# Moving transpositions and loads in a fused linear-attention and SwiGLU kernel

## The chip, the cores and the metric

The kernel runs on one core of one Trainium2 chip. The core has a TensorE (matrix multiplications, which also does transpositions by multiplying with an identity matrix), a VectorE, a ScalarE and a GpSimd engine, and a SyncE that only issues transfers. Transfers run on 16 DMA engines, which serve the queues of all issuers. In the profile's rows the engines are called PE (PEld is its loading of stationary operands), DVE, ACT, POOL and SP.

The metric is device time in microseconds; smaller is better.

## The reference

Linear attention with cosine weights, followed by a gated feed-forward network. There are 8 batches of 8 heads, 576 positions and 64 columns a head, so 4608 tokens of 512 columns; the feed-forward width is 1536.

```python
def phi(x, c, s):
    r = np.maximum(x, 0.0)
    return np.concatenate([r * c, r * s], axis=-1)
q_p = phi(q, cos_w, sin_w)
k_p = phi(k, cos_w, sin_w)
kv = np.einsum('bhsf,bhsd->bhfd', k_p, v)
z = np.sum(k_p, axis=2)
num = np.einsum('bhsf,bhfd->bhsd', q_p, kv)
den = np.einsum('bhsf,bhf->bhs', q_p, z)[..., None] + 1e-06
attn = num / den                       # then x: one row of 512 a token

rms = np.sqrt(np.mean(x * x, axis=-1, keepdims=True) + 1e-06)
xn = x / rms * rms_g
g = xn @ w_gate
out = (g * (1.0 / (1.0 + np.exp(-g))) * (xn @ w_val)) @ w_out
```

## The kernel before

**Tiles and blocks.** The first 512 positions of batch b are block b, four x tiles of 128 tokens (j = 0 to 3). The last 64 positions of all eight batches are gathered two batches at a time ("tails", four "pairs") into block 8. The blocks run in the order 0 to 6, 8, 7.

**A block of the feed-forward network.** For each of 12 column groups n (steps 0 to 11), `gval_step` multiplies the transposed normed x (`xnT`, 512 tokens wide) with 128 columns of the gate weights into a bank `psG[n % 2]` and of the value weights into `psV[n % 2]`, four matmuls each. `gval_h` applies silu on ScalarE and multiplies on VectorE into `hT`. Then four output steps (12 to 15), `out_step`, multiply one token tile each with the output weights (12 matmuls), copy the result and store it over SP's queue.

**The attention of later batches** runs between these steps. The function `at(blk, n, where, f, *args)` puts a call into a slot of a block's step: "pe" is ahead of the step's matmuls, "mid" in the middle of an output step, "pre" after the matmuls, "post" at the end. Within a slot, calls run in the order in which they were entered; each engine and each queue works in program order. For a batch these calls are:

- `load_kv`, `load_q`: transfers from DRAM into one of five buffers `raw`. Batches 0 to 2 hold k and v in one layout, batches 3 to 7 (`wide`) in another, with all heads of 112 rows in one transfer and the last rows in a second.
- `k_phi`, `q_phi`: half of each on VectorE, half on ScalarE. `v_cast`: v to bfloat16.
- `q_tr_pe` with `q_tr_evac`, or `q_tr_dma`: q's features transposed into `qpT`, on TensorE with a copy out of the bank, or by a DMA transposition on SP's queue.
- `kvz_pe`, `kvz_evac`: the sums over positions.
- `nd_pe`, `nd_post`, `x_sq`, `x_norm`: one tile's numerator and denominator on TensorE, the division on VectorE, the mean square on ScalarE (and a power on GpSimd), the normed tile `xn` on VectorE.
- `x_tr_pe` with `x_tr_evac`, or `x_tr_dma`: `xn` transposed into `xnT`, four 128 x 128 transpositions on TensorE and a copy, or a DMA transposition on SP's queue.
- `load_q_tails`, `q_tails_phi`, `q_tails_tr_dma`, `nd_tails_pe`: the same for a pair's tails.

**Block 0** is special, since nothing is there to run behind. Its attention comes first; then the twelve column groups are worked on in eight `units`, as x tiles become ready: units 0 to 3 take tile 0 or 1 alone with four column groups each (128 tokens wide), units 4 to 7 take tiles 2 and 3 as a pair with two column groups each (256 wide). `unit_mm(i, w)` does a unit's 16 (or 8) matmuls for the gate or the value weights, `unit_silu` and `unit_h` the rest. Column groups 8 to 11 are then done for all four tiles in `gval_step`. `out_first` does the output of block 0: 48 matmuls, and after every sixth a slot, so that steps 12 to 15 with "pe" and "mid" hold batch 1's `nd_pe`, `x_norm` and transpositions (the table `X1`, lines 744 to 757). `filler` matmuls on a tile of zeros stand where TensorE would otherwise have nothing in the opening.

**Queues.** GpSimd's queue carries the opening loads: q0, v0, the weights, k1, q1, v1, and, from block 0's column steps, k2, v2 and q2. SP's queue carries k0, and from the end of block 0 on the output stores, the DMA transpositions and the loads of batch 3 on. A DMA transposition takes its place in SP's order behind the loads and stores ahead of it.

**Lines that the change and the prediction touch:** `load_kv` (106), the units (606 to 709), batch 1's x tiles (744 to 757), the loads of batch 2 (731 to 737), the tails (785 to 796), the loads of batches 3 to 7 (797 to 804).

Of the kernel before, what the change touches and what calls it, by code (L numbers as in the profile page):

```python
# [17 lines left out]
def kernel(  # L18
# [11 lines left out]
    nc = tc.nc  # L30
    B, H, S, D = q.shape
    DM = H * D
    DFF = moe_w_gate.shape[1]
    P = 128
    TB = 512
    HP = H // 2
# [4 lines left out]
    NDT = DM // P  # L41
# [5 lines left out]
    V, A, G = nc.vector, nc.scalar, nc.gpsimd  # L47
# [10 lines left out]
    psG = [ps.tile([P, 512], FP32, name=f"psG{i}") for i in range(2)]  # L58
    psV = [ps.tile([P, 512], FP32, name=f"psV{i}") for i in range(2)]
    psC = [ps.tile([P, 512], FP32, name=f"psC{i}") for i in range(2)]  # L60
# [8 lines left out]
    def kv_rows(src, b, hps):  # L69
        return src[b, 2 * hps[0] : 2 * hps[1], :, :].rearrange(  # L70
            "(hp hh) (s c) d -> (hh s) hp (c d)", hh=2, c=NC
        )

    def wide(b):
        return b > 2
# [4 lines left out]
    def kv_rows5(src, b, r0, r1):  # L80
        part = src[b, :, 0 : NC5 * (KP - 1), :].rearrange(
            "h (p c) d -> p h (c d)", c=NC5
        )[r0 : min(r1, KP - 1)]
        return bass.AP(part.tensor, part.offset, [[NC5 * D, r1 - r0]] + list(part.ap)[1:])
# [6 lines left out]
    def raw_tile(which, b):  # L91
        if (which, b) not in raw:
            t = ring.tile([P, H * NC5 * D], FP32, name="raw", tag="raw")
            raw[(which, b)] = t
        return raw[(which, b)]

    def raw_kv(which, b):
        t = raw_tile(which, b)
        if wide(b):
            return t[:, :].rearrange("p (h e) -> p h e", h=H)  # L100
        return t[:, 0 : HP * NC * D].rearrange("p (hp e) -> p hp e", hp=HP)
# [4 lines left out]
    def load_kv(which, b, hps=(0, HP), eng=nc.sync):  # L106
        src = k if which == "k" else v
        if not wide(b):
            return eng.dma_start(
                out=raw_kv(which, b)[:, hps[0] : hps[1], :], in_=kv_rows(src, b, hps)  # L110
            )
        last = KP if b < B - 1 else KP - 1
        for r0, r1 in ((0, KM), (KM, last)):
            eng.dma_start(out=raw_kv(which, b)[r0:r1, :, :], in_=kv_rows5(src, b, r0, r1))
        if last < KP:
            eng.dma_start(
                out=raw_kv(which, b)[last:KP, :, :].rearrange("p h (c d) -> p h c d", d=D),
                in_=src[b, :, S - 1 : S, :].rearrange("h s d -> s h d").unsqueeze(2)
                .to_broadcast([1, H, NC5, D]),
            )  # L120
# [19 lines left out]
    for c0, c1 in ((0, 4), (4, NC)):  # L140
        nc.sync.dma_start(
            out=raw_kv("k", 0)[:, :, c0 * D : c1 * D],
            in_=kv_rows(k, 0, (0, HP))[:, :, c0 * D : c1 * D],
# [24 lines left out]
    wg = one.tile([P, NDT, DFF], BF16, name="wg")  # L168
    wv = one.tile([P, NDT, DFF], BF16, name="wv")
# [42 lines left out]
    part, left = [], 1e-6  # L212
    for i in range(3):
        m, e = math.frexp(left)
        part.append(math.ldexp(round(m * 256), e - 8))
        left -= part[i]
        G.memset(eps_rows[32 * i : 32 * i + 32, :], part[i] / 32)
    load_kv("k", 1, eng=G)
    load_w(wg, moe_w_gate, 8, NNT)

    def g_spread(bank, t):
# [12 lines left out]
        out=th[:, 0:NTAB], in0=fidx[:, :], scalar1=S - 1.0, scalar2=ang,  # L234
        op0=ALU.min, op1=ALU.mult,
    )
    for c0, c1, less in ((0, 9, 576.0), (13, 14, 64.0)):
        V.tensor_scalar(
            out=th[64:128, c0:c1], in0=fidx[64:128, c0:c1], scalar1=-less, scalar2=ang,
# [3 lines left out]
        out=th[:, NTAB : 2 * NTAB], in0=th[:, 0:NTAB], scalar1=math.pi / 2.0,  # L243
# [4 lines left out]
        out=sel[:, :, :], in_=ident[0:4, 0:4].unsqueeze(2).to_broadcast([4, NDT, P])  # L248
# [17 lines left out]
    xnT = [one.tile([P, NDT, TB], BF16, name=f"xnT{i}") for i in range(2)]  # L266
# [6 lines left out]
    def copy(eng, o, i):  # L273
        if eng is A:
            A.copy(out=o, in_=i)  # L275
        else:
            eng.tensor_copy(out=o, in_=i)  # L277
# [201 lines left out]
    def nd_post(b, j):  # L479
        nd_rec(b, j)  # L480
        nd_div(b, j)
# [22 lines left out]
    def x_dst(b, j):  # L504
        if j == 4:
            t, col = xnT_tail, b // 2
        else:
            t, col = xnT_of(b), j
        return t[:, :, col * P : (col + 1) * P]
# [4 lines left out]
    def x_tr_pe(b, j, bank, ts=(0, NDT)):  # L514
        xn = xn_of[(b, j)]
        dst = bank.bitcast(BF16).rearrange("p (t s) -> p t s", s=P)
        for t in range(*ts):
            nc.tensor.transpose(dst[:, t, :], xn[:, t * P : (t + 1) * P], ident[:, :])

    def x_tr_evac(eng, b, j, bank, ts=(0, NDT)):  # L520
        dst = bank.bitcast(BF16).rearrange("p (t s) -> p t s", s=P)
        copy(eng, x_dst(b, j)[:, ts[0] : ts[1], :], dst[:, ts[0] : ts[1], :])
# [48 lines left out]
    def filler(n, bank):  # L571
        for _ in range(n):
            nc.tensor.matmul(
                bank[:, :], lhsT=warm[:, 0:P], rhs=warm[:, :], start=True, stop=True
            )
# [30 lines left out]
    units = [(j, j + 1, 4 * i, 4 * i + 4) for i in range(2) for j in range(2)]  # L606
    units += [(2, 4, n, n + 2) for n in range(0, 8, 2)]
    sg_of = {}

    def unit_mm(i, w, by_rows=False):  # L610
        j0, j1, n0, n1 = units[i]
        bank = (psG if w is wg else psV)[i % 2]
        width = (j1 - j0) * P
        todo = [(n, t) for n in range(n0, n1) for t in range(NDT)]
        if by_rows:
            todo = [(n, t) for t in range(NDT) for n in range(n0, n1)]
        for n, t in todo:
            nc.tensor.matmul(  # L618
                bank[:, (n - n0) * width : (n - n0 + 1) * width],
                lhsT=w[:, t, n * P : (n + 1) * P],  # L620
                rhs=xnT[0][:, t, j0 * P : j1 * P],
                start=(t == 0 and (n == n0 or not by_rows)),
                stop=(t == NDT - 1 and (n == n1 - 1 or not by_rows)),
                skip_group_check=by_rows,
            )

    def unit_silu(i):
        sg_of[i] = four.tile([P, TB], FP32, name="sg", tag="sg")
        A.activation(out=sg_of[i][:, :], in_=psG[i % 2][:, 0:TB], func=AF.Silu)

    def unit_h(i):
        j0, j1, n0, n1 = units[i]
        V.tensor_tensor(
            out=hT[:, n0:n1, j0 * P : j1 * P],
            in0=psV[i % 2][:, 0:TB].rearrange("p (n s) -> p n s", n=n1 - n0),
            in1=sg_of[i][:, :].rearrange("p (n s) -> p n s", n=n1 - n0), op=ALU.mult,
        )
# [22 lines left out]
    x_sq(0, 1)  # L660
    load_q(1, eng=G)
    load_kv("v", 1, eng=G)
    x_norm(0, 0, (0, HALF))
    x_norm(0, 0, (HALF, DM))
# [5 lines left out]
    q_tr_evac(A, 0, 3, qbank[3])  # L670
    x_norm(0, 1)
    nd_post(0, 2)
    filler(2, psG[1])
    unit_mm(0, wg, by_rows=True)
    x_tr_pe(0, 1, psC[0])
    x_tr_evac(V, 0, 1, psC[0])
    unit_mm(0, wv)
    x_sq(0, 2)
    load_wo(0, 4)
# [13 lines left out]
    x_tr_evac(V, 0, 2, psC[1])  # L693
    unit_silu(2)
    unit_h(0)
    unit_mm(3, wg)
    x_tr_pe(0, 3, psC[0])
    x_tr_evac(V, 0, 3, psC[0])
    unit_silu(3)
    unit_h(1)  # L700
    unit_mm(4, wg)
    for i in range(2, 4):
        unit_mm(i, wv)
        unit_h(i)
    unit_silu(4)
    unit_mm(5, wg)
    unit_mm(4, wv)
    unit_silu(5)
# [4 lines left out]
    def at(blk, n, where, f, *args):  # L713
        slots.setdefault((blk, n), {}).setdefault(where, []).append((f, args))
# [19 lines left out]
    at(0, 10, "post", load_kv, "v", 2, (0, HP), G)  # L734
    at(0, 12, "pe", kvz_pe, 1)
    at(0, 12, "pe", kvz_evac, A, 1)
    at(0, 11, "post", load_q, 2, (0, 4), G)

    def x_tr(b, j, bank):
        x_tr_pe(b, j, bank)  # L740
# [3 lines left out]
    X1 = (  # L744
        ((12, "mid"), (13, "pe"), (14, "pe")),
        ((13, "pe"), (13, "mid"), (14, "mid")),
        ((13, "mid"), (14, "pe"), (15, "pe")),
        ((14, "pe"), (14, "mid"), (15, "mid")),
    )
# [3 lines left out]
        if j:  # L753
            at(0, *X1[j - 1][1], x_norm, 1, j - 1)
    at(0, *X1[3][1], x_norm, 1, 3)
    for j in range(4):
        at(0, *X1[j][2], x_tr, 1, j, psV[j % 2])
    for nb in range(2, B):
        b = nb - 1
        first = nb == 2  # L760
# [16 lines left out]
        for j in range(4):  # L777
            n = ((6, 8, 10, 12) if first else (4, 6, 8, 10))[j]
# [5 lines left out]

    for pair in range(4):
        b = 2 * pair or 3
        if pair == 0:
            at(1, 15, "post", load_q_tails, 0)
        at(b, 3, "post", q_tails_phi, V, pair, 0)
        at(b, 3, "post", q_tails_phi, A, pair, 1)  # L790
        at(b, 3, "post", q_tails_tr_dma, pair)
        at(b, 12, "pe", nd_tails_pe, pair)
        at(b, 12, "pre", nd_post, 2 * pair + 1, 4)
        at(b, 12, "post", x_sq, 2 * pair + 1, 4)
        at(b, 13, "post", x_norm, 2 * pair + 1, 4)
        at(b, 13, "post", x_tr_dma, 2 * pair + 1, 4)
    for nb in range(3, B):
        b = nb - 2
        late = b == 1
        at(b, 0, "post", load_kv, "k", nb)  # L800
        at(b, 5 if late else 3, "post", load_kv, "v", nb)
        at(b, 8 if late else 6, "post", load_q, nb)
        if nb % 2 == 1:
            at(b, 9, "post", load_q_tails, nb // 2)

    def gval_step(blk, n):
        run(blk, n, "pe")
# [86 lines left out]
```

## Time and profile before

| | |
|---|---|
| median of 3 runs | 324.93 us (324.65 to 325.04) |
| profiled execution | 324.66 us |
| its span, first to last instruction | 322.9 us |
| granted clock of TensorE | 0.999 |
| transfers | 53.37 MB, mean 165 GB/s |
| out stage of block 0, first matmul | 42.87 us |
| block 1, first matmul | 55.80 us |
| block 2, first matmul | 89.22 us |

The page of a profile gives busy times by engine, the chain of work that ended last, groups of like instructions and the transfers. A timeline row has a start, a duration, the engine, the line, the operation, the tile written and those read, the shape and a count; in brackets stands how long the engine was idle before it, and what ended that. A row of stretches has the stretch, its length, the busy time and count of each engine (PE, PEld, DVE, ACT, POOL), TensorE's granted clock, the mean busy share of the DMA engines, and GB/s. A row of waits has who waited for whom, the total in microseconds, how many times, and the longest. In all of them the times are microseconds from the span's start.

Some sizes of transfers, issue to landing, by the page: loads of k, v and q on SP's queue 8.4, 8.5 and 8.9 us (1120, 1120 and 1024 KB); on GpSimd's queue 19.4, 16.1 and 16.1 us; x transpositions on SP's queue 7.8 us; output stores 2.4 us.

### The profile page before, as it was taken

What the parts mean: (1) busy time and instruction counts of PE and PEld (TensorE: products, weight loads), DVE (VectorE), ACT (ScalarE), POOL (GpSimd) and SP (SyncE); (2) the same over time, 40 slices, a digit from 0 to 9 for tenths busy, and PEclk for the clock granted to TensorE, in tenths of its full rate; (3) what the DMA queues carried; (4) which work ended last, traced back from release to release, by engine and by line L of the source; (5) the groups of instructions that cost most, each with busy time, mean ns of one, the idle gap of its engine ahead of it and who ended that gap; (6) DMA issues with size and microseconds to landing.
All of it is one profiled execution on the core that took longest, in us unless ns stands there. A gap on an engine that the chain in (4) does not pass through costs nothing.

```text
span 322.9 us, 6078 instructions
## 1 busy us (share of the span) xinstructions
PE 315.6 (98%) x2312; PEld 163.5 (51%) x2348; DVE 185.5 (57%) x380; ACT 164.9 (51%) x319; POOL 40.6 (13%) x78
## 2 busy tenths in 40 slices
PE   8999999999999999999999999999999999999996
PEld 3688565544454445444544445444544444444444
DVE  8875958767636773676457745781577034204410
ACT  5664766744665457445754575446644333223321
POOL 9771302001001100011001000110011000000000
PEclk9999999999999999999999999999999999999999
DMA  7999996999789966998699959994822300041002
GB/s 229 233 266 272 283 327 240 230 200 240 149 156 232 234 190 161 195 233 202 175 198 214 210 148 207 202 217 141 119 49 48 117 32 0 2 98 31 3 32 97
DMA packets 77627, 53.37 MB, mean 165 GB/s; under 512 B 50410, under 2 KB 71326, under 8 KB 77598
## 3 DMA queue, kind: packets, MB, share of 16 engines
q1 hardware_dynamic: 70374, 39.81, 58.2%
q0 software_dynamic: 7216, 13.17, 16.5%
q8 instruction: 18, 0.29, 0.4%
q14 instruction: 11, 0.09, 0.1%
q10 hardware_dynamic: 8, 0.00, 0.0%
HBM read 37.83 MB, written 9.44 MB: 146 GB/s over the span
## 4 chain that ended last, share of the span: by engine, by line
PE 93%; DMA 2%; DVE 2%; issue 1%; POOL 0%; ACT 0%; ACTq 0%; POOLq 0%
PE psV L528 27%; PE psC L551 27%; PE psG L528 26%; PE psA L421 2%; DMA raw<-in_q_dram 2%; PE psG L551 2%; PE psV L618 2%; PE psA L359 2%; PE psG L618 1%; PE psA L366 1%; DVE xn L499 1%; PE psV L335 0%; PE psA L446 0%; DVE xt L471 0%; PE psG L402 0%
## 5 line engine op out<-in xcount | busy, mean ns | idle before, releaser
L548 DVE TENSOR_TENSOR hT<-psV,sg 128x512 bf16<-128x512 f32 x100 | 68.9, 689 | 102.1 <-PE psV L528 65.0
L547 ACT ACTIVATE sg<-psG 128x512 f32<-128x512 f32 x100 | 59.2, 592 | 62.5 <-PE psG L528 54.6
L528 PE MATMUL psV<-xnT,wv 128*128 128x512 bf16 x345 | 89.8, 379 | 0.6
L528 PE MATMUL psG<-xnT,wg 128*128 128x512 bf16 x338 | 88.6, 379 | 0.6 <-issue 0.2
L551 PE MATMUL psC<-wo,hT 128*128 128x512 bf16 (+1 forms) x398 | 88.6, 376 | 0.5
L551 PEld LDWEIGHTS <-hT 128*128 128x128 bf16 x456 | 42.9, 98 | 47.1
L528 PEld LDWEIGHTS <-wv 128*128 128x128 bf16 x400 | 39.1, 98 | 47.2
L528 PEld LDWEIGHTS <-wg 128*128 128x128 bf16 x400 | 37.0, 98 | 39.8
L492 POOL TENSOR_TENSOR rs<-ms,mhalf 128x1 f32<-128x1 f32 x36 | 19.8, 550 | 195.6 <-ACT scr L487 195.6
L275 ACT COPY osb<-psC 128x512 f32<-128x512 f32 x32 | 18.7, 585 | 50.0 <-PE psC L551 46.1
L487 ACT ACTIVATE scr<-xt 128x513 bf16<-128x513 f32 x36 | 22.8, 635 | 25.2 <-DVE xt L471 25.1
L499 DVE SCALAR_TENSOR_TENSOR xn<-xt,rs,gb 128x512 bf16<-128x512 f32 (+1 forms) x37 | 26.9, 730 | 10.3 <-POOL rs L492 10.3
L281 ACT ACTIVATE kp<-raw,tab 128x256 bf16<-128x256 f32 (+2 forms) x51 | 28.8, 607 | 2.3 <-DMA raw<-in_k_dram 2.3
L471 DVE TENSOR_TENSOR xt<-psA,rec 128x512 f32<-128x512 f32 x36 | 24.9, 692 | 1.2
L281 ACT ACTIVATE qp<-raw,tab 128x512 bf16<-128x512 f32 x32 | 22.6, 714 | 0.8 <-DMA raw<-in_q_dram 0.8
L283 DVE TENSOR_SCALAR kp<-raw,tab 128x256 bf16<-128x256 f32 (+2 forms) x53 | 20.4, 429 | 0.3 <-DMA raw<-in_k_dram 0.3
L283 DVE TENSOR_SCALAR qp<-raw,tab 128x512 bf16<-128x512 f32 x31 | 15.5, 506 | 0.3 <-DMA raw<-in_q_dram 0.3
L421 PEld LDWEIGHTS <-qpT 128*128 128x128 bf16 x224 | 10.5, 97 | 6.6 <-issue 0.5
L528 PE MATMUL psV<-xnT_tail,wv 128*128 128x512 bf16 x48 | 12.3, 379 | 0.1
L528 PE MATMUL psG<-xnT_tail,wg 128*128 128x512 bf16 x46 | 12.1, 379 | 0.1
L421 PE MATMUL psA<-kvzs,qpT 128*128 128x65 bf16 x224 | 11.4, 193 | 0.0
L277 DVE CAST vv<-raw 116x1280 bf16<-116x1280 f32 (+1 forms) x13 | 10.5, 807 | 0.0
(97 smaller groups left out, 181.2 us busy)
## 6 DMA issues: line engine op xcount, KB each, us to landing
out_dram<-osb SPq DMA_DIRECT2D x31, 256.0 KB, 2.4
raw<-in_k_dram SPq DMA_DIRECT2D x5, 1120.0 KB, 8.4
raw<-in_v_dram SPq DMA_DIRECT2D x5, 1120.0 KB, 8.5
raw<-in_q_dram SPq DMA_DIRECT2D x5, 1024.0 KB, 8.9
raw<-in_k_dram POOLq DMA_DIRECT2D x2, 1152.0 KB, 19.4
raw<-in_v_dram POOLq DMA_DIRECT2D x2, 1152.0 KB, 16.1
raw<-in_q_dram POOLq DMA_DIRECT2D x2, 1024.0 KB, 16.1
wg<-in_moe_w_gate_dram POOLq DMA_DIRECT2D x3, 512.0 KB, 14.2
```

The lines of the kernel that those rows point to most:

```text
L275: A.copy(out=o, in_=i)
L281: A.activation(out=out_ap, in_=in_ap, func=AF.Relu, scale=scale)
L283: eng.tensor_scalar(out=out_ap, in0=in_ap, scalar1=scale, scalar2=0.0, op0=ALU.mult, op1=ALU.max)
L421: nc.tensor.matmul(heads[:, g, hp, :], lhsT=qpT[:, h, j * P : (j + 1) * P], rhs=kvzs[b][:, g, hp * E : (hp + 1) * E], start=True, stop=True,)
L471: V.tensor_tensor(out=xt[:, 0:DM].rearrange("p (hp g d) -> p g hp d", g=2, d=D), in0=heads[:, :, :, 0:D], in1=rec[:, :, :].unsqueeze(3).to ...
L487: A.activation(out=scr[:, :], in_=xt[:, 0 : DM + 1], func=AF.Square, scale=1.0 / math.sqrt(DM), accum_out=ms[:, :],)
L492: G.tensor_tensor(out=rs[:, :], in0=ms[:, :], in1=mhalf[:, :], op=ALU.pow)
L499: V.scalar_tensor_tensor(out=xn_of[(b, j)][:, c], in0=x_of[(b, j)][:, c], scalar=rs_of[(b, j)][:, :], in1=gb[:, c], op0=ALU.mult, op1=ALU. ...
L528: nc.tensor.matmul(bank[:, cols[0] : cols[1]], lhsT=w[:, t, n * P : (n + 1) * P], rhs=x[:, t, cols[0] : cols[1]], start=(t == 0), stop=(t ...
L547: A.activation(out=sg[:, :], in_=g[:, 0:TB], func=AF.Silu)
L548: V.tensor_tensor(out=hT[:, n, :], in0=v[:, 0:TB], in1=sg[:, :], op=ALU.mult)
L551: nc.tensor.matmul(bank[:, 0 : cols[1] - cols[0]], lhsT=hT[:, n, j * P : (j + 1) * P], rhs=wo[:, n, cols[0] : cols[1]], start=(n == 0), st ...
```

## The change

1. **Block 0's units.** The gates of unit 3 (tile 1, column groups 4 to 7) are cut after 12 of 16 matmuls, and x tile 3's transposition stands in the cut; its copy goes from VectorE to ScalarE. The gates of unit 4 (tiles 2 and 3) are done one tile at a time (`unit_tile`, 8 matmuls of 128 columns each), with the value matmuls of units 2 and 3 in between and after. One of two filler matmuls ahead of unit 0 is gone.
2. **Batch 1's x tiles** 0, 1 and 2 are transposed by DMA on SP's queue, in the slot of their `x_norm`, and not on TensorE; tile 3 stays on TensorE. q2's load moves from GpSimd's queue at step 11 to SP's queue, to the middle of output step 14, behind the three transpositions.
3. **Batch 3's loads** move within block 1: k from step 0 to 4, v from 5 to 7, q from 8 to 11. Batch 2's x tiles are transposed by DMA at steps 7, 9, 11 and 13 of the same block.
4. **Tails.** Pair 0's rows load at step 9 of block 2 (before: step 15 of block 1), pair 1's at step 0 of block 2 (before: step 9 of block 1); pair 1's features and transposition go from step 3 to step 5.
5. **v of batches 4 to 7** is loaded in two halves of the heads (and the last rows), as `v_cast` reads it.

```diff
+        parts = ((0, H),) if which == "k" or b == 3 else ((0, HP), (HP, H))
         for r0, r1 in ((0, KM), (KM, last)):
-            eng.dma_start(out=raw_kv(which, b)[r0:r1, :, :], in_=kv_rows5(src, b, r0, r1))
+            for h0, h1 in parts if r0 == 0 else ((0, H),):
+                eng.dma_start(
+                    out=raw_kv(which, b)[r0:r1, h0:h1, :],
+                    in_=kv_rows5(src, b, r0, r1)[:, h0:h1, :],
+                )
...
-    def unit_mm(i, w, by_rows=False):
+    def unit_mm(i, w, by_rows=False, part=(0, 16)):
...
-        for n, t in todo:
+        for n, t in todo[part[0] : part[1]]:
...
+    def unit_tile(i, j):
+        j0, j1, n0, n1 = units[i]
+        for n in range(n0, n1):
+            c = ((n - n0) * (j1 - j0) + j - j0) * P
+            for t in range(NDT):
+                nc.tensor.matmul(
+                    psG[i % 2][:, c : c + P], lhsT=wg[:, t, n * P : (n + 1) * P],
+                    rhs=xnT[0][:, t, j * P : (j + 1) * P],
+                    start=(t == 0), stop=(t == NDT - 1),
+                )
...
-    filler(2, psG[1])
+    filler(1, psG[1])
...
-    unit_mm(3, wg)
+    unit_mm(3, wg, part=(0, 12))
     x_tr_pe(0, 3, psC[0])
-    x_tr_evac(V, 0, 3, psC[0])
+    x_tr_evac(A, 0, 3, psC[0])
+    unit_mm(3, wg, part=(12, 16))
     unit_silu(3)
     unit_h(1)
-    unit_mm(4, wg)
-    for i in range(2, 4):
-        unit_mm(i, wv)
-        unit_h(i)
+    unit_tile(4, 2)
+    unit_mm(2, wv)
+    unit_h(2)
+    unit_tile(4, 3)
     unit_silu(4)
+    unit_mm(3, wv)
+    unit_h(3)
     unit_mm(5, wg)
...
-    at(0, 11, "post", load_q, 2, (0, 4), G)
...
-    for j in range(4):
-        at(0, *X1[j][2], x_tr, 1, j, psV[j % 2])
+    for j in range(3):
+        at(0, *X1[j][1], x_tr_dma, 1, j)
+    at(0, *X1[3][2], x_tr, 1, 3, psV[1])
+    at(0, *X1[3][1], load_q, 2)
...
-        if pair == 0:
-            at(1, 15, "post", load_q_tails, 0)
-        at(b, 3, "post", q_tails_phi, V, pair, 0)
-        at(b, 3, "post", q_tails_phi, A, pair, 1)
-        at(b, 3, "post", q_tails_tr_dma, pair)
+        at(*((2, 9), (2, 0), (3, 9), (5, 9))[pair], "post", load_q_tails, pair)
+        n = 5 if pair == 1 else 3
+        at(b, n, "post", q_tails_phi, V, pair, 0)
+        at(b, n, "post", q_tails_phi, A, pair, 1)
+        at(b, n, "post", q_tails_tr_dma, pair)
...
-        late = b == 1
-        at(b, 0, "post", load_kv, "k", nb)
-        at(b, 5 if late else 3, "post", load_kv, "v", nb)
-        at(b, 8 if late else 6, "post", load_q, nb)
-        if nb % 2 == 1:
-            at(b, 9, "post", load_q_tails, nb // 2)
+        for which, n in zip("kvq", (4, 7, 11) if b == 1 else (0, 3, 6)):
+            if which == "q":
+                at(b, n, "post", load_q, nb)
+            else:
+                at(b, n, "post", load_kv, which, nb)
```

## The prediction, made before the run

> **What bounds the kernel now.** I read the page first, then the waits of the TensorE, then the timeline around the edited places. The page's busy times and its chain of waits:
>
> ```profile
> PE 315.6 (98%) x2312; PEld 163.5 (51%) x2348; DVE 185.5 (57%) x380; ACT 164.9 (51%) x319; POOL 40.6 (13%) x78
> ...
> PE 93%; DMA 2%; DVE 2%; issue 1%; POOL 0%; ACT 0%; ACTq 0%; POOLq 0%
> ```
>
> TensorE is busy for 98% of the span and is 93% of the chain. So an edit pays only if it takes work off TensorE or closes one of its few gaps, and it costs only if it opens a new gap. The TensorE's waits, whole span, say where the gaps are:
>
> ```profile
> PE psC L573 <- DVE warm L154: 1.2, 1, 1.2
> PE psG L618 <- DVE xnT L277: 0.5, 1, 0.5
> PE psA L335 <- ACT qp L281: 0.2, 1, 0.2
> ```
>
> The first and third lie in the opening 10 us, which the change doesn't touch. The second is one wait in the units of block 0. From 56 us on the same view has a single wait of 0.2 us: there is nothing left to gain in blocks 1 to 8, and everything the change moves there can only lose. The wait in the timeline:
>
> ```profile
> 23.56 0.39 PE L518 MATMUL psC<-ident,xn 128*128 128x128 bf16 x4
> 23.76 0.60 ACT L629 ACTIVATE sg<-psG 128x512 f32<-128x512 f32 x1 [0.52 <-PE psG L618]
> 23.83 0.74 POOL L179 DMA_DIRECT2D wo<-in_moe_w_out_dram  x1 [0.71 <-DMA wv<-in_moe_w_val_dram]
> 24.01 0.41 DVE L277 COPY xnT<-psC 128x512 bf16<-128x512 bf16 x1
> 24.34 0.68 DVE L633 TENSOR_TENSOR hT<-psV,sg 128x512 bf16<-128x512 f32 x1
> 24.47 0.11 PEld L618 LDWEIGHTS <-wg 128*128 128x128 bf16 x2 [0.70 <-DVE xnT L277]
> ```
>
> TensorE transposes x tile 3 at 23.56, has nothing until VectorE has copied it, and starts the pair's gates at 24.48. Start to start, a 128-column matmul is 0.056 us here (32 in 1.79 us on the chain), a 256-column one 0.109 (8 in 0.87), a 512-column one 0.216.
>
> **Part 1, units of block 0.** Old: the four transposes end at 23.56 + 4 x 0.056 = 23.79, and the next matmul starts at 24.48: 0.69 us lost. New, from the gates of unit 3 at 22.67: 12 matmuls to 23.34; transposes to 23.56 (xn of tile 3 is done: VectorE's x_norm runs 22.41 to 23.16); the last 4 to 23.79; tile 2's half of unit 4, 8 to 24.23; 16 value matmuls of unit 2 to 25.13; tile 3's half to 25.57; 16 of unit 3 to 26.47. Unit 5 began at 27.15, so 0.68 us are gained, the 16 narrow matmuls in place of 8 wide ones (0.89 for 0.87) included. What now comes last: tile 2's copy is done at 23.49, before 23.79; unit 2's values need psV[0], free when hT ends at 23.41 + 0.68 = 24.09, against 24.23; its wv columns landed 16.0 us after an issue at 7.53, at 23.5 (the release of POOL at 23.83 above); tile 3's copy, now 0.57 us on ScalarE as its like at 51.87, ends near 24.4, against 25.13. The smallest margin is 0.14 us. ScalarE takes the copy into a gap.
>
> Does the 0.68 us reach the end of block 0? Loads set some times there: q1, issued at 17.45, lands 17.0 later at 34.5, and ScalarE's q_phi, at 34.82 before, would start at 34.1, so it waits 0.4; the silu behind it sat 0.52 idle, so nothing passes on. The wo rows 4 to 7 land at 22.33 + 20.0 = 42.3 and are needed at 42.9. I take all of it; bounds 0 and 0.69.
>
> **Part 2, one filler matmul less** (0.216 us of TensorE). Behind it come the first gates, 17.46 to 18.35, then the transposes of x tile 1, whose xn VectorE makes from 17.52 to 18.27. Gates that start at 17.25 end at 18.14 and the transposes wait until 18.33: the filler covered a wait, the gain is 0.02. Bounds 0 and 0.22.
>
> **Part 3, batch 1's tiles 0 to 2 by DMA.** Each tile cost TensorE 4 x 0.056 = 0.22 us (49.725 to 49.946 between the neighbours' starts). Three make 0.67 us, all on the path. Two ScalarE copies (0.57) and one of VectorE (0.42) go too, hidden before. Added are three transposes on SP's queue, 1.2 us of issue each, and q2's load moves from POOL's queue to behind them on SP. Block 1's first matmul reads all four tiles. It started at 55.80 and would start at 55.80 - 0.70 - 0.67 = 54.43. The x_norms of the tiles:
>
> ```profile
> 47.65 0.74 DVE L499 SCALAR_TENSOR_TENSOR xn<-xt,rs,gb 128x512 bf16<-128x512 f32 x1
> 49.35 0.74 DVE L499 SCALAR_TENSOR_TENSOR xn<-xt,rs,gb 128x512 bf16<-128x512 f32 x1
> 51.05 0.74 DVE L499 SCALAR_TENSOR_TENSOR xn<-xt,rs,gb 128x512 bf16<-128x512 f32 x1
> ```
>
> With 0.70 off, SP issues at 47.7, 49.4 and 51.1: the third has 3.3 us. How long does one take? Before, the last tile of batch 2 was issued at 85.29; the DMA engines were quiet by 87.30, and block 2 read it at 89.0 without a wait:
>
> ```profile
> 85.29 1.24 SPq L512 DMA_TRANSPOSE xnT<-xn  x1
> ...
> 85.30:86.30 1.00, 1.00 (x6) 0.49 (x5) 1.00 (x4) 0.14 (x1) 0.00 (x0) 1.00 0.60 215
> 86.30:87.30 1.00, 1.00 (x7) 0.41 (x5) 1.00 (x3) 0.47 (x1) 0.00 (x0) 1.00 0.80 178
> 87.30:88.20 0.90, 0.90 (x6) 0.43 (x5) 0.42 (x2) 0.90 (x3) 0.00 (x0) 1.00 0.00 0
> ```
>
> So 2.0 us for the data, some 2.5 until it can be used (estimate), with at most 0.8 us of the engines' time. The first tile meets v2, which POOL issues at 38.59 and which lands 13.1 later, at 51.7. If v2 shut the transposes out until then, three would need 3 x 0.8 = 2.4 us: 54.1, and about 54.6 in use, a stall of 0.2. If they share, the third is there at 53.6, stall 0. Upper bound: a transpose issued at 104.55 behind a 1.1 MB load took 7.4, which makes 58.5, a stall of 4.1. I take 0.1: v2 is in another queue and gone by 52, so the quiet row is the nearest.
>
> [...] No row of before shows a transpose beside another queue's load. [...]
>
> The fourth tile stays on TensorE. VectorE's order is then x_norm (from 51.9), three k_phi, the copy out of bank 1, the copy of the tile, ending near 54.4: level with 54.43, so 0 to 0.1.
>
> q2 is issued near 52.4 instead of 39.35. Alone it needs 1 MB at some 340 GB/s, 3 us, plus starting: 57 to 58; ScalarE asks for it at 59.88 - 1.37 = 58.5. With the page's median for q on SP (8.9) it lands at 61.3; the silu behind it then ends near 62.6 while its bank is needed at 64.07 - 1.37 = 62.7. Free up to there.
>
> **Part 4, batch 3's loads** go to steps 4, 7 and 11 of block 1. k3 leaves the four qpT transposes' way (7.17 us of SP for four, 61.35 on). It lands near 73, used at 79.9; v3 near 79, used at 83.2. q3 now comes after tile 2's transpose, near 80.3 instead of 74.19, and ahead of tile 3's, near 83.9. At 3 to 4.5 us it lands by 84.8; the last transpose then ends by 86.6, and block 2 starts at 89.0 - 1.37 = 87.6. VectorE waits some 0.5 us for q3, with 4.04 us idle before its next hT. Cost 0, with 1 us of margin; bound 2.9 (the last rival).
>
> **Part 5, tails and halves of v.** The tail rows of pair 1 are loaded at block 2's start and used five steps (8.6 us) later, those of pair 0 four steps and an out stage before use; both transposes have over 5 us until their step 12. The v loads of batches 4 to 7 become three issues, 0.5 us more of SP, which idles there. Cost 0; without that idle, 0.5 us of later landing with margins of 5 us and more.
>
> **Sum.** -0.68 - 0.02 - 0.67 + 0.1 = -1.27. The profiled execution took 324.66 (span 322.9), so 323.4; the median of the runs, 324.93, is 0.27 higher, so 323.66. I say 323.5.
>
> **Rivals.**
> A, the third x tile is late for block 1. For: 3.3 us of room, and SP stood 4.3 us in a transpose that followed another (of the row that shows 8.63 us for three issues at 106.49, two are 1.2 each by the others' rate, which leaves over 4). Against: no load is ahead of it in its own queue. A stall of 0.5 to 1.3 leaves 323.9 to 324.8; I write 324.3. Chance 0.16.
> B, block 0's shift is absorbed by a load or by VectorE before 42.9: only the transposes are gained, 324.93 - 0.67 = 324.2. For: VectorE has no idle time from 37.6 to 42.4. Against: its inputs all move with TensorE. This is also the case that the reorder doesn't do what it says. Chance 0.07.
> C, slower: q3 blocks batch 2's last tile at block 2's start. Place: SP's queue at 80 to 87 us. With the page's median 8.9 us q3 lands at 89.2, tile 3 is usable 1.3 later at 90.5, and TensorE waits 2.9: 324.93 - 1.27 + 2.9 = 326.6. It decides from q3 taking over 6 us, and makes the kernel slower from 7.3. For: the median itself. Against: those 8.9 us were mostly spent behind a v load; here v3 has landed. Chance 0.13.
>
> **How the numbers follow.** The forecast (323.0 to 323.9) has 0.64. The range reaches to A and part of C: 322.9 to 325.2. A measurement of this kernel can tell about 0.2%, 0.65 us, so faster is below 324.28: forecast 0.64, half of A, half of B: 0.76. Same: the rest of A and B, 0.11. Slower: C, 0.13.
>
> **What would show it.** Right: no wait of TensorE on xnT near 24 and unit 5 near 26.5; block 1's first matmul near 54.5; block 2's near 87.7; no new wait of TensorE after. Wrong: a wait on a DMA of xnT at 54 or 88, or a VectorE wait on q2 of over 3 us.

## The result, and the profile after

The changed kernel takes 326.65 us (median of 7 runs, 325.38 to 326.83), the kernel before 325.04 beside it (324.65 to 325.22). The ratio is 1.0042, 95% interval 1.0028 to 1.0056: slower, by more than the 0.2% that can be told apart. The forecast was 323.5, range 322.9 to 325.2, with 0.13 on slower.

The profiled execution took 326.83 us, span 325.1, against a span of 322.9 before. In the new file the two streaming products stand at L533 and L556 (before L528 and L551), the units at L623 and L638 (before L618), the transposition of x by DMA at L517. Busy time and the chain of waits, from the page of the changed kernel:

```profile
PE 315.5 (97%) x2307; PEld 162.9 (50%) x2343; DVE 184.1 (57%) x378; ACT 165.2 (51%) x318; POOL 39.9 (12%) x77
...
PE 88%; DMA 8%; POOL 2%; issue 1%; DVE 0%; ACT 0%; POOLq 0%; ACTq 0%
```

TensorE is as busy as before (315.5 against 315.6 us) in a span 2.2 us longer, and DMA has gone from 2% to 8% of the chain: by lines, 4% is wv's load in the opening, 2% the transposition of tail rows of q (qpTt), 2% that of x (xnT). So the time went into waits, and the two that are new are on transpositions. The TensorE's waits of the changed kernel from 10 us on (total, times, longest):

```profile
PE psG L533 <- DMA xnT<-xn: 1.2, 1, 1.2
PE psA L451 <- DMA qpTt<-qp: 0.8, 1, 0.8
PE psA L340 <- ACT qp L286: 0.8, 1, 0.8
```

The third is in the opening (0.2 before), and so is a further new one of 0.3 us on wv's load. The first two are new and come late; the wait on tile 3 in the units (0.5 before) is gone. Here is the place of each in TensorE's timeline of the changed kernel: unit 3's gates with the transposition amid them, unit 5, the starts of block 1 and block 2, and the tail rows at step 12 of block 2.

```profile
23.95 0.83 PE L623 MATMUL psG<-xnT,wg 128*128 128x128 bf16 x12
24.62 0.39 PE L523 MATMUL psC<-ident,xn 128*128 128x128 bf16 x4
...
27.75 0.49 PE L623 MATMUL psG<-xnT,wg 128*128 128x256 bf16 x3
...
43.47 1.47 PE L556 MATMUL psG<-wo,hT 128*128 128x512 bf16 x5
...
55.75 1.04 PE L533 MATMUL psG<-xnT,wg 128*128 128x512 bf16 x4
...
90.53 1.02 PE L533 MATMUL psG<-xnT,wg 128*128 128x512 bf16 x4 [1.18 <-DMA xnT<-xn]
...
114.46 0.44 PE L451 MATMUL psA<-kvzs,qpTt 128*64 128x65 bf16 x16 [0.85 <-DMA qpTt<-qp]
```

Of the kernel before, unit 3's gates and unit 5 (its block starts stand in the table of its profile):

```profile
22.67 1.06 PE L618 MATMUL psG<-xnT,wg 128*128 128x128 bf16 x16
...
27.15 1.04 PE L618 MATMUL psG<-xnT,wg 128*128 128x256 bf16 x8
```

Read differences between rows, since this execution opened late: q and v of the first batch landed some 0.9 us later than in the profile before (k 0.3), and unit 3's gates start at 23.95, not 22.67. From unit 3's gates to unit 5 it is 27.75 - 23.95 = 3.80 us (before 27.15 - 22.67 = 4.48). From the first output matmul of block 0 to block 1 it is 12.28 (before 55.80 - 42.87 = 12.93). From block 1 to block 2 it is 34.78, where it was 89.22 - 55.80 = 33.42. So the units give 0.68 us, the tiles give 0.65, block 1 loses 1.36, and the tails 0.85 more. With the late opening: 1.28 - 0.68 - 0.65 + 1.36 + 0.85 = 2.16 of the span's 2.2.

What made block 2 wait is read from SP's timeline. First the changed kernel, then the kernel before:

```profile
49.02 4.85 SPq L517 DMA_TRANSPOSE xnT<-xn  x3
53.99 0.51 SPq L128 DMA_DIRECT2D raw<-in_q_dram  x1
...
61.35 7.16 SPq L323 DMA_TRANSPOSE qpT<-qp  x4
68.62 1.10 SPq L116 DMA_DIRECT2D raw<-in_k_dram  x2
...
74.14 1.03 SPq L116 DMA_DIRECT2D raw<-in_v_dram  x2
76.58 4.93 SPq L517 DMA_TRANSPOSE xnT<-xn  x2
81.61 0.54 SPq L128 DMA_DIRECT2D raw<-in_q_dram  x1
...
85.27 1.26 SPq L517 DMA_TRANSPOSE xnT<-xn  x1
```

```profile
57.17 1.00 SPq L114 DMA_DIRECT2D raw<-in_k_dram  x2
61.35 7.17 SPq L318 DMA_TRANSPOSE qpT<-qp  x4
68.63 1.09 SPq L114 DMA_DIRECT2D raw<-in_v_dram  x2
...
74.19 0.52 SPq L123 DMA_DIRECT2D raw<-in_q_dram  x1
```

The four transpositions of q take SP the same 7.17 us with k3 ahead of them or not. k3 now comes where v3 was (68.6), v3 where q3 was (74.1), and q3 7.4 us later. The trace's landings go with that:

| transfer | issued, landed before | issued, landed after |
|---|---|---|
| q2 | 39.35, 54.60 (GpSimd's queue) | 53.99, 60.58 |
| k3 | 57.17, 65.6 | 68.62, 76.67 |
| v3 | 68.63, 77.2 | 74.14, 83.04 |
| q3 | 74.19, 80.7 | 81.61, 88.38 |
| x tile 3 of batch 2 | 85.29, 87.71 | 85.27, 90.49 |

Tile 3 is issued at the same moment and lands 2.8 us later, 2.1 us behind q3. Block 2 starts at 90.53, as soon as it is there.

Between 61 and 92 us all transfers on SP's queue land in the order of their issue, in both traces. So each can be given the time from the landing ahead of it to its own. In the changed kernel k3 takes 6.25 us so (behind the last transposition of q at 70.42), v3 5.86, tiles 1 and 2 1.84 and 0.51, q3 2.99, two output stores 1.90 together, tile 3 0.21. Before, the last transposition of q landed at 70.43 with k3 already through. So k3, which cost those transpositions nothing where it was, now adds its time to all that lands after them, and q3 and tile 3 come last (pair 1's rows, which took 2.35 us between tiles 1 and 2 before, have left that place). With q3 behind it, tile 3 would land near 87.7 by this reckoning (an estimate: 85.39 for tile 2, 1.90 for the stores, at least 2.4 from its own issue); no kernel with that order was measured. VectorE shows q3's lateness too: it idles 2.63 us for it before its first q_phi of batch 3 at 88.40.

### The profile page after: what moved, and what is told of

It reads as the page before. It is cut to its first block, busy times and chain, and to the rows that moved or that the text cites. A ratio compares the mean times of both kernels' runs of the same rounds, so it can differ in the third digit from the quotient of the medians.

```text
span 325.1 us, 6072 instructions
## 1 busy us (share of the span) xinstructions
PE 315.5 (97%) x2307; PEld 162.9 (50%) x2343; DVE 184.1 (57%) x378; ACT 165.2 (51%) x318; POOL 39.9 (12%) x77
## 4 chain that ended last, share of the span: by engine, by line
PE 88%; DMA 8%; POOL 2%; issue 1%; DVE 0%; ACT 0%; POOLq 0%; ACTq 0%
PE psV L533 26%; PE psG L533 25%; PE psC L556 24%; DMA wv<-in_moe_w_val_dram 4%; PE psV L623 2%; DMA qpTt<-qp 2%; PE psA L426 2%; PE psG L556 2%; PE psA L364 2%; PE psG L623 2%; DMA xnT<-xn 2%; PE psA L371 1%; POOL raw L128 1%; PE psA L451 0%; POOL vv L208 0%
## 5 line engine op out<-in xcount | busy, mean ns | idle before, releaser
L552 ACT ACTIVATE sg<-psG 128x512 f32<-128x512 f32 x100 | 59.2, 592 | 62.6 <-PE psG L533 55.1
L533 PE MATMUL psV<-xnT,wv 128*128 128x512 bf16 x345 | 89.8, 379 | 0.6
L533 PE MATMUL psG<-xnT,wg 128*128 128x512 bf16 x337 | 88.5, 379 | 1.9 <-DMA xnT<-xn 1.2
L556 PE MATMUL psC<-wo,hT 128*128 128x512 bf16 (+1 forms) x399 | 88.5, 376 | 0.5
L556 PEld LDWEIGHTS <-hT 128*128 128x128 bf16 x456 | 42.9, 98 | 47.6
L533 PEld LDWEIGHTS <-wv 128*128 128x128 bf16 x400 | 39.1, 98 | 47.2
L533 PEld LDWEIGHTS <-wg 128*128 128x128 bf16 x400 | 37.0, 98 | 41.2 <-issue 1.5
L288 DVE TENSOR_SCALAR qp<-raw,tab 128x512 bf16<-128x512 f32 x31 | 14.7, 480 | 3.4 <-DMA raw<-in_q_dram 3.4
L533 PE MATMUL psV<-xnT_tail,wv 128*128 128x512 bf16 x48 | 12.3, 379 | 0.1
L533 PE MATMUL psG<-xnT_tail,wg 128*128 128x512 bf16 x46 | 12.1, 379 | 0.1
```

Of the source, the lines that this page charges most:

```text
L288: eng.tensor_scalar(out=out_ap, in0=in_ap, scalar1=scale, scalar2=0.0, op0=ALU.mult, op1=ALU.max)
L533: nc.tensor.matmul(bank[:, cols[0] : cols[1]], lhsT=w[:, t, n * P : (n + 1) * P], rhs=x[:, t, cols[0] : cols[1]], start=(t == 0), stop=(t ...
L552: A.activation(out=sg[:, :], in_=g[:, 0:TB], func=AF.Silu)
L556: nc.tensor.matmul(bank[:, 0 : cols[1] - cols[0]], lhsT=hT[:, n, j * P : (j + 1) * P], rhs=wo[:, n, cols[0] : cols[1]], start=(n == 0), st ...
```

## The experiments

Three readings were tried against each other: the loads' new steps cost the time; q2's new place does; or the transpositions by DMA do. "Block 1" in the table is from block 1's first matmul to block 2's in the profiled execution, and "out of block 0" from block 0's first output matmul to block 1's.

| kernel | median us (runs) | ratio, 95% | out of block 0 | block 1 |
|---|---|---|---|---|
| before | 325.04 (7) | | 12.93 | 33.42 |
| changed | 326.65 (7) | 1.0042, 1.0028 to 1.0056 | 12.28 | 34.78 |
| e1_loads_back | 329.54 (6) | 1.014, 1.0105 to 1.0176 | 12.28 | 38.07 |
| e2_tails_back | 328.01 (12) | 1.0076, 1.0054 to 1.0097 | 12.28 | 36.57 |
| e3_loads_tails_back | 328.55 (11) | 1.0094, 1.0063 to 1.0124 | 12.28 | 39.54 |
| e4_units_only | 324.35 (12) | 0.9971, 0.9953 to 0.9988 | 12.92 | 33.43 |
| e6_loads_only | 328.91 (6) | 1.0111, 1.0087 to 1.0136 | 12.92 | 36.10 |
| e7_tails_only | 325.28 (12) | 1.001, 1.0 to 1.002 | 12.93 | 33.43 |
| f1_q2_back | 327.37 (6) | 1.007, 1.0054 to 1.0087 | 14.02 | 34.53 |
| f2_units_tiles | 326.76 (6) | 1.0051, 1.0035 to 1.0067 | 14.28 | 34.59 |
| f3_q2_alone | 328.64 (6) | 1.0106, 1.008 to 1.0132 | 12.93 | 35.76 |
| f4_two_tiles | 325.84 (12) | 1.0022, 1.0012 to 1.0033 | 13.88 | 33.43 |
| g1_k3_between | 324.93 (12) | 0.9995, 0.9981 to 1.0008 | 12.28 | 35.14 |
| g2_q2_late_pool | 327.98 (6) | 1.008, 1.005 to 1.0111 | 12.30 | 37.38 |

The ratios go by the kernel before as it ran on the same chip (medians 324.93, 325.1 and 324.93 in the three groups).

**The changed kernel with parts put back.** e1: batch 3's loads back at their old steps. e2: the tail rows back at theirs. e3: both.

```diff
-        for which, n in zip("kvq", (4, 7, 11) if b == 1 else (0, 3, 6)):
+        for which, n in zip("kvq", (0, 5, 8) if b == 1 else (0, 3, 6)):
```

and for the tail rows

```diff
-        at(*((2, 9), (2, 0), (3, 9), (5, 9))[pair], "post", load_q_tails, pair)
-        n = 5 if pair == 1 else 3
+        at(*((1, 15), (1, 9), (3, 9), (5, 9))[pair], "post", load_q_tails, pair)
+        n = 3
```

> The changed kernel with batch 3's loads back at steps 0, 5 and 8 of block 1; all else as changed. Queue theory (the loss of block 2 is q3's load ahead of x tile 3 of batch 2 on SP's queue): the 1.3 us wait at block 2's first matmul is gone. If the 0.9 us wait on qpTt at step 12 of block 2 is a consequence of the same backlog, it goes too and the median falls by 2.2 us to about 324.5; if that wait belongs to the moved tails, it stays and the median falls by 1.3 to about 325.4. Rival (the loss lies in the opening, where TensorE's unit 3 came 1.3 us later than before): block 2's wait may go, but the opening stays 1.3 us late in the profile, and the median stays near 325.4 even without both waits.

> The changed kernel with the tails back (pair 0 loaded at step 15 and pair 1 at step 9 of block 1, features at step 3); batch 3's loads stay at 4, 7, 11. Queue theory: the wait at step 12 of block 2 goes (minus 0.9), and the wait at block 2's first matmul stays or grows, since pair 1's rows come onto SP's queue at step 9 of block 1, ahead of q3: 1.3 to 2.5 us. Median 325.5 to 327. Rival (the opening): as changed in the opening, 1.3 us late.

> The changed kernel with both batch 3's loads and the tails back: the units, the three x tiles by DMA with q2 on SP, and v's halves remain. Queue theory: no wait at block 2's start nor at step 12; the gain forecast for units and tiles appears, 1.3 us less than before: about 323.7. Rival (the opening): 1.3 us late in the opening, so no faster than before, about 325.

All three are worse than the whole change. In e1 and e3 the wait of block 2 on x is gone and a larger one stands inside block 1, on the transpositions of q. From the TensorE's waits of e1, and from its SP timeline:

```profile
PE psA L426 <- DMA qpT<-qp: 2.8, 1, 2.8
```

```profile
56.56 1.37 SPq L116 DMA_DIRECT2D raw<-in_k_dram  x2
60.46 10.60 SPq L323 DMA_TRANSPOSE qpT<-qp  x4
```

k3 is issued at 56.6 as before, but q2, which now lands in SP's own queue near 60, stands ahead of it, and the four transpositions take SP 10.6 us where they took 7.2. So once q2 has moved, k3 must not stand ahead of them: the loads' new steps answer q2's. In e2 the tail rows, issued between the x tiles of batch 2, push q3 and tile 3 back, and block 2 waits 3.0 us instead of 1.2. So the tail rows' move, too, takes part of a cost away that the change itself made. All three came out above what was expected (324.5 to 325.4, 325.5 to 327 and 323.7).

**Single parts on the kernel before.** e4 has the units and the filler alone, e6 the loads' steps alone, e7 the tail rows' steps alone; everything else is as before. Their edits are the matching hunks of the change as its diff shows them, e4's those of the units and of the filler, e6's the loop over k, v and q, e7's the two lines of the tail rows' steps; v is loaded in one piece in all three.

> The kernel before with the change of block 0's units and the filler alone. Theory: 0.7 us less than before, 324.3, with the out stage of block 0 starting 0.7 us earlier relative to unit 0. Rival (the opening comes late because the filler or the units moved): unit 3 comes 1.3 us later than before in the profile and the median is 325.5 or above.

> The kernel before with batch 3's loads alone at steps 4, 7 and 11 of block 1; q2 on GpSimd's queue, tiles on TensorE, pair 1's tails loaded at step 9 of block 1, ahead of q3. If the new places are too late by themselves: a wait on xnT at block 2's first matmul of 1 to 3 us, 326 to 328. If only q2's load ahead of them made them late: no such wait, 325.0 within 0.3.

> The kernel before with the tails alone moved (pair 0 loaded at step 9 and pair 1 at step 0 of block 2, pair 1's features and transposition at step 5). If the move is too late by itself: a wait of 0.7 to 1.4 us on qpTt at step 12 of block 2, 325.7 to 326.4. If the backlog of block 1 made it late: no wait, 325.0 within 0.3.

e4 is the best kernel of this study: 324.35, 0.6 us under before, with no new wait. In its TensorE timeline unit 3's gates and unit 5 stand 3.80 us apart:

```profile
22.79 0.83 PE L623 MATMUL psG<-xnT,wg 128*128 128x128 bf16 x12
...
26.59 1.04 PE L623 MATMUL psG<-xnT,wg 128*128 128x256 bf16 x8
```

e6 shows the loads' price without anything else: a wait of 2.5 us at block 2's start, on the same tile (SP issues it at 85.91), behind the same load (issued at 82.09). From TensorE's timeline of e6:

```profile
91.80 1.02 PE L533 MATMUL psG<-xnT,wg 128*128 128x512 bf16 x4 [2.51 <-DMA xnT<-xn]
```

With the loads at 4, 7 and 11 the wait comes whether or not x tiles go by DMA and wherever q2 is (1.2 us in the changed kernel, 2.5 in e6); in e7 and e4, without that edit, block 1 has its old length. e7 shows the tail rows' new place alone:

```profile
112.29 0.44 PE L451 MATMUL psA<-kvzs,qpTt 128*64 128x65 bf16 x16
```

TensorE takes them without a wait, but only just: their transposition landed at 112.25. Before, it landed at 105.48, 6.7 us ahead of its use. So the new place uses up the whole margin, and anything that comes later still makes TensorE wait: 0.85 us in the changed kernel, 0.6 in f1, 1.2 in e1, all with this place; e2 and e3, with the old one, have no such wait. What came later in those three isn't settled. Their rows themselves did not (both landed by 8.6 us after block 2's start in the changed kernel, by 9.4 in e7), so a backlog from block 1 is not shown. v of batch 4 is in halves in all three and whole in e7, and its halves were not tried apart; but in e4, which has v whole, the transposition of q that follows batch 4's k also lands later than before (16.8 us after block 2's start, against 15.3).

**The tiles and q2.** f1: the changed kernel with q2 back in GpSimd's queue, at its old step. f2: before, with the units and three x tiles by DMA, q2 where it was. f4: the same with two tiles by DMA. f3: before, with q2 alone moved to SP, behind the first store of block 0. g2: units and three tiles, q2 in GpSimd's queue but late, behind the last x_norm. Loads, tails and v are as before in all of them but f1.

q2 back in f1, f2 and f4, and late in GpSimd's queue in g2:

```diff
-    at(0, *X1[3][1], load_q, 2)
+    at(0, 11, "post", load_q, 2, (0, 4), G)
```

```diff
-    at(0, *X1[3][1], load_q, 2)
+    at(0, *X1[3][1], load_q, 2, (0, 4), G)
```

Two tiles in f4, and q2 in f3 against the kernel before:

```diff
-    for j in range(3):
-        at(0, *X1[j][1], x_tr_dma, 1, j)
-    at(0, *X1[3][2], x_tr, 1, 3, psV[1])
+    for j in range(4):
+        if j < 2:
+            at(0, *X1[j][1], x_tr_dma, 1, j)
+        else:
+            at(0, *X1[j][2], x_tr, 1, j, psV[j % 2])
```

```diff
-    at(0, 11, "post", load_q, 2, (0, 4), G)
+    at(0, 14, "post", load_q, 2)
```

> The changed kernel with q2's load alone back on GpSimd's queue at step 11 of block 0; the three x tiles by DMA, the new places of batch 3's loads and of the tails stay. Theory (q2's 1 MB on SP's queue pushes everything behind it in block 1 by its own 3 us, and comes out wherever the queue's first deadline is): the waits on xnT at block 2's start and on qpTt at step 12 of block 2 go or shrink to under 0.5 us, and the median falls by 1.5 to 2.2 us, to 324.5 to 325.2. Rival 1 (the new places of batch 3's loads and of the tails are too late by themselves): both waits stay, 326.5. Rival 2 (x tiles by DMA beside GpSimd's loads are late): a new wait on xnT at block 1's start of 0.5 us or more.

> The kernel before with the units, the filler and the three x tiles of batch 1 by DMA; q2 stays on GpSimd's queue and batch 3's loads, the tails and v stay as before. Theory: nothing is pushed, both parts' gains come, 1.35 us less than before: 323.6, with a stall of at most 0.3 us at block 1's start. Rival (transposes beside q2 and v2 in GpSimd's queue wait for them, until q2's landing near 54.6 us): the third tile is usable near 55.2 and TensorE stalls 0.8 us or more at block 1's start: 324.4 or above.

> As the run with the units and three tiles by DMA and q2 on GpSimd's queue, but only x tiles 0 and 1 by DMA; tiles 2 and 3 on TensorE. Theory: the second tile is issued 1.7 us earlier than the third, so no stall at block 1's start whatever GpSimd's queue does: 0.68 + 0.44 = 1.1 us less than before, 323.8. It beats the run with three tiles if that one stalls by over 0.22 us.

> The kernel before with one edit: q2's load on SP's queue behind the first output store of block 0 (near 54 us), in place of GpSimd's queue at step 11. Tiles, units, loads of batch 3 and tails as before. Theory: k3 and the four qpT transposes queue behind q2, TensorE waits about 3 us on qpT in the middle of block 1, and the median rises by 2.5 to 3.5 us, to 327.5 to 328.5. Rival (the x tiles' transposes are what fills SP's queue): no wait, 325.

> As before with the units and three x tiles by DMA, but q2's load on GpSimd's queue behind the last x_norm of batch 1 (near 53 us), so neither ahead of the three transposes nor ahead of k3 in SP's queue; batch 3's loads at 0, 5, 8, tails as before, v whole. If a transpose waits for loads of another queue that were issued before it: the three x tiles land as in the changed kernel (the third near 55), no wait at block 1's start; the qpT transposes then meet k3 and q2, and a wait of 1 to 3 us in block 1 stays, 325 to 327. If it is the SP queue's order alone that counts: no wait, 323.6.

f1, f2 and f4 answer what the trace of before could not: how long a transposition takes beside another queue's load. Three issues, at 48 to 52 us in f2, landed at 55.96, 56.44 and 56.87; q2 had landed at 55.50. In f1 they landed at 55.12, 55.61 and 56.04, behind q2 at 54.64; in f4 at 55.78 and 56.21, behind q2 at 55.33. Each time the first lands 0.45 to 0.48 us after q2's last byte and the next follow 0.4 to 0.5 apart. From issue that is 7.7 us for the first and 5.2 for the third in f2 (issued at 48.27 and 51.7), where in the changed kernel, with at most the last packets of v2 beside them, the second and third tile took 2.48 and 2.47. f4, with two tiles, starts block 1 at 56.34, after a wait of 1.2 us that the view puts down to VectorE's kp; the second tile had landed 0.13 us before. Stretches of f2 (PE, PEld, DVE, ACT, POOL busy, clock, DMA share, GB/s):

```profile
49.00:51.00 2.00, 2.00 (x17) 0.97 (x16) 1.93 (x6) 0.72 (x2) 0.59 (x2) 1.00 1.02 364
...
53.00:54.00 1.00, 1.00 (x9) 0.61 (x8) 1.00 (x5) 1.00 (x3) 0.00 (x0) 1.00 0.71 82
54.00:55.00 1.00, 1.00 (x6) 0.29 (x3) 0.95 (x3) 0.84 (x3) 0.00 (x0) 1.00 1.73 56
55.00:56.00 1.00, 0.14 (x1) 0.00 (x0) 0.82 (x2) 0.70 (x2) 0.00 (x0) 1.00 1.11 179
```

From 49 to 51 v2's end and q2 moved at 364 GB/s, and no packet of SP's queue moved, although the first two tiles were issued at 48.27 and 49.97. From 52 to 53, with v2 landed at 52.07, packets of both queues moved, 321 of SP's and 44 of GpSimd's. From 53 to 55 q2's rest and the transpositions are both there, the engines are taken up (0.71 and 1.73) and only 82 and 56 GB/s move; TensorE stands still from 55.1. The wait is in the TensorE's waits of f2, with a second one that follows from it:

```profile
PE psG L533 <- DMA xnT<-xn: 1.9, 1, 1.9
PE psA L426 <- DMA qpT<-qp: 1.0, 1, 1.0
```

That the transpositions would share with the load and be done in time was an estimate of the prediction's. In f2 packets of the two queues did move in the same stretch, but only from 52 on, and the landings speak against the rest of the estimate: they came one after another, the first 0.46 us behind the end of the load.

So the tiles by DMA need q2 out of the way, and f3 tells what that costs by itself: q2 on SP at 54 puts k3 and the four transpositions of q behind it, block 1 is 2.34 us longer, with a wait of 2.2 on qpT. In g2 q2 is late in the other queue and the wait is the same kind (2.1). Out of block 0, g2 has the tiles' gain in full (12.30).

**A version with the loads in between.** g1: units, three tiles and q2 on SP as in the change; batch 3's loads at steps 2, 6 and 9, so that k3 stands between the second and third transposition of q; tail rows of pair 1 loaded at step 13 of block 1, with features and transposition at step 3 again; v in one piece.

```diff
-        for which, n in zip("kvq", (4, 7, 11) if b == 1 else (0, 3, 6)):
+        for which, n in zip("kvq", (2, 6, 9) if b == 1 else (0, 3, 6)):
...
-        at(*((2, 9), (2, 0), (3, 9), (5, 9))[pair], "post", load_q_tails, pair)
-        n = 5 if pair == 1 else 3
+        at(*((2, 9), (1, 13), (3, 9), (5, 9))[pair], "post", load_q_tails, pair)
+        n = 3
```

> The changed kernel's units, three x tiles by DMA and q2 on SP, with batch 3's loads at steps 2, 6 and 9 (k3 between the second and the third qpT transposition), tails at step 3 again with pair 1's rows loaded at step 13 of block 1, v whole. If the order of the loads is the trouble and SP's queue has room in block 1: no wait over 0.5 us, 323.6 to 324.3, faster than before. If the queue has no room (q2's 3 us must come out somewhere): a wait of 1 us or more on qpT in block 1 or on xnT at block 2's start, 325 or above.

It takes 324.93, the same as before within its interval, and 0.6 us more than e4. Its profiled execution (325.53, above its median) waits 1.3 us at block 2's start; its lowest run is 323.61. So three x tiles by DMA pay for their own queueing at best in the orders measured. Which of g1's edits took the 1.7 us back, the loads' steps, the tail rows' place or v in one piece, was not measured apart.

## Why the prediction was wrong

**Part 1 and Part 2, right.** -0.68 -0.02 was forecast for units and filler. The trace has 3.80 us from unit 3's gates to unit 5, as worked out, and e4 is 0.58 us faster than before (324.93 - 324.35). The filler was not tried apart from the units. Rival B, an absorbed shift, falls: the nine variants that have the units begin block 0's output at 42.0 to 42.7, those without them at 42.8 to 42.9. The profile of the changed kernel has 43.47, for its late opening. e1, e2, e3 and f1 differ from it only in calls from step 11 of block 0 on; there batch 0's q landed at 8.4 to 9.0 (9.5 in the changed kernel's profile) and block 0's output began at 42.0 to 42.6. So the late opening looks like that one execution's; the changed kernel was not profiled again. Without it the profile's own terms come to +0.88 us (-0.68 - 0.65 + 1.36 + 0.85), while the medians differ by 1.6: some 0.7 us of the slowdown stay open.

**Part 3, right in sum.** Forecast -0.67 + 0.1 to block 1's start, measured 12.28 - 12.93 = -0.65. The third tile was forecast usable at 53.6 to 54.6; it was issued 1.5 us later and landed 2.47 us after (2.5 estimated). Of the two readings about the first tile, neither held whole: its packets moved beside v2's last ones (419 and 17 from 50 to 51), yet it landed at 52.77, 0.5 us behind v2. It cost nothing only because v2 was done by 52.25. q2 landed at 60.58, between the forecast 57 to 58 and the 61.3 by the page's median, and no wait followed from that directly. Rival A did not come.

**Part 4 is the step that failed: cost 0.** The forecast was that k3 "lands near 73", "v3 near 79" and that q3, issued near 80.3, "lands by 84.8" at 3 to 4.5 us. Measured: 76.67, 83.04 and 88.38. The last transposition was to end by 86.6 and landed at 90.49. Of these differences of 3.6 to 4.0 us, 1.3 come from block 1's start (55.75, forecast 54.43); 2.3 to 2.7 are the queue's. Two things were taken wrongly. That k3 "leaves the four qpT transposes' way" was counted as good, but they took 7.16 us, as before (7.17): nothing was saved there, and k3, v3 and q3 each moved down a place behind them. And the loads were priced too low: q3 at its size over 340 GB/s (the profile of before moved 336 from 51 to 52), although every load of that stretch in the profile of before, among transpositions in the same queue, took 6.5 to 8.5 us from issue to landing (k3 8.4, v3 8.5, q3 6.5). Now k3 took 8.05, v3 8.90 and q3 6.77. q3's own part was indeed 2.99 us; the rest went by because v3 and two transpositions had to land first (83.04, 84.88, 85.39, against an issue at 81.61). Against rival C the prediction had put that the page's 8.9 us "were mostly spent behind a v load; here v3 has landed": it had not. In e6 this edit alone makes block 1 2.68 us longer.

What happened is rival C in mechanism and place: q3 blocks batch 2's last tile at block 2's start. Its point of decision (q3 over 6 us, slower from 7.3) was set almost where it fell, its wait (2.9) is 1.2 in the change, and its time, 326.6, is the measured one; that agreement is partly luck, since another 0.85 us came from the tails and the opening was late. With the 6.77 us that q3 took, C's own reckoning gives no loss yet.

**Part 5, cost 0, wrong in the change, and right alone by a hair.** The forecast gave the tails' transposition over 5 us until step 12. e7 has no wait (325.28, ratio 1.001), but it leaves 0.04 us. In the change TensorE waits 0.85 us for it. The margin was not worked out through SP's queue, in which batch 4's k and v and an x tile stand ahead of it. The halves of v were never priced by a run of their own.

**The sum as a method.** Alone on the kernel before, the parts move the median by -0.6 (e4), +4.0 (e6), +3.5 (f3) and +0.35 (e7); four of the six runs of e6 and three of the six of f3 have a mean clock of 0.994 or 0.995, as with the half clock told of below. The tiles on top of the units add 2.2 (f2 is 1.66 above before, e4 0.58 below). The sum of these is 9.5, and the whole is +1.6, with v's halves in it, which have no price. The tiles need q2 moved, q2 needs k3 moved, k3's move needs the tail rows moved: each edit pays for the one ahead of it, and no price of one edit says what the whole costs.

## What to carry to other kernels

Loads that moved in SP's queue moved what landed behind them (k3, v3 and q3 a place lower, x tile 3 of batch 2 landed at 90.49 and not 87.71): follow the queue, landing by landing, to its last urgent transfer. Bytes over bandwidth gave q3's own part (3.0 of 6.8 us) and not what stood ahead of it; and k3 and v3 took some 6 us each of the queue, not the 3.4 of 1120 KB at 340 GB/s. Before taking 0.22 us of transposition off TensorE, ask whether the DMA transposition has a queue and a stretch to itself; here three tiles pushed a load (q2) out of its place, and each place tried for it cost more than the tiles gave, or as much. Where edits depend on each other, try them alone: the one that stood by itself (e4) was the only clear gain.

## What the runs showed of the hardware that was not expected

**The first transposition did not land ahead of another queue's load that was issued before it.** It landed 0.45 to 0.48 us behind q2's end in f1, f2 and f4, and 0.52 behind v2's in the changed kernel (52.77 and 52.25). q2 itself landed later: 3.4 to 3.5 us behind v2 in the first three, 2.9 before.

**A wait of 2.5 us cost 4 in e6.** Stretches of e6 around block 2's start; the clock is the third figure from the end:

```profile
90.00:92.00 2.00, 0.20 (x1) 0.13 (x2) 1.69 (x4) 2.00 (x4) 0.00 (x0) 1.00 1.12 304
92.00:94.00 2.00, 2.00 (x8) 0.78 (x7) 0.00 (x0) 1.24 (x3) 0.00 (x0) 0.74 1.07 261
94.00:96.00 2.00, 2.00 (x6) 0.73 (x5) 1.09 (x2) 0.07 (x1) 0.00 (x0) 0.50 0.82 168
96.00:98.00 2.00, 2.00 (x39) 1.40 (x38) 0.79 (x2) 1.21 (x2) 0.00 (x0) 0.91 0.93 176
```

After the wait of 2.51 us TensorE's granted clock falls to half (0.50 from 94 to 96); the loss is 2 x (0.26 + 0.50 + 0.09) = 1.7 us of full-speed time, so the half clock lasted 3.4 us. The wait and the clock account for e6's time: 328.91 is 4.0 above before, of which about 2.5 are the wait and 1.7 the clock. It does not come in each execution: e2's twelve runs with a mean clock of 1.0 took 326.16 to 327.54 (four), those with 0.995 took 327.71 to 328.62 (eight). Waits up to 1.9 us (f2, f1, the changed kernel) were not followed by a fall in their profiles (mean clock 1.000); f3's 2.2 was not (0.998), g2's 2.1 was (0.993). So the length of the wait alone does not tell which is followed by one.
